# Output stores issued by ACT, attention's ACT work pinned behind the FFN's, the x split pinned on ACT and DVE, and the local part moved in two reading transfers

## The chip, the cores and the metric

One core of one Trainium2 chip runs one program. Its five engines work beside each other, each through a list of its own: TensorE (PE) multiplies, VectorE (DVE), ScalarE (ACT) and GpSimd (POOL) work on elements, SyncE (SP) issues the transfers. The metric is device time in microseconds of one execution, the median of the runs; lower is better.

## The reference

The input is q, k, v of shape (8, 8, 576, 64) and the weights of an FFN. Attention has a far and a local part, whose sum is the FFN's input.

```
q_d, k_d, v_d = mean of q, k, v over groups of 4 positions        # 144 positions
out_up    = repeat(softmax(q_d k_d^T / 8) v_d, 4)                 # far part
out_local = softmax(q k^T / 8 where |i - j| < 4) v                # local part
x = (out_up + out_local) as 4608 tokens x 512
h = x @ w_in ; r = max(h, 0) ; g = s * r*r + b ; out = g @ w_out   # 512 -> 2048 -> 512
```

All of it is float32. The kernel splits x, both weights and g into a high and a low part, and makes each product of three matmuls: high by high, low by high, high by low.

## The kernel before, in words

**Tiles and steps.** The 4608 tokens are 18 tiles of 256, the hidden dimension is 8 parts of 256. One pair (tile t, part p) is a step; from tile 3 on, tile t's steps are numbers 8t to 8t+7. A step has four pieces of work: G (`products1`, L771), 24 matmuls of x by w_in into one bank `ph`, of which the first reads `xh` and the second `xl`; R (`upper`, L786 to L788) on ACT, relu, square and the high part `gh`; V (`lower`, L793) on DVE, the low part `gl`; and H (`products2`, L852 to L854), 12 matmuls into the accumulators `po`. In the third of three steps gh and gl are halves of one tile named `gb`. V reads `ph` last, and from tile 3 on two banks take turns, so G of step k+2 can begin only when V of step k is done. At a tile's end `evict_half` (L826) reads `po` on DVE into `os`, and a store (L829) goes out on SP.

**Stages.** A written list (`PLAN`) sets the order up to step 27 and holds the attention of the first three batches. From step 28 on a loop takes steps in pairs: three matmuls of G, H pieces, the rest of G, R and V (`finish`), one H piece, `advance`, then the whole G of the odd step, its R and V, and six H pieces (18 matmuls), `advance`, and `split`. PE's own order is chained by hand. `advance` pulls as many yields from the attention of batches 3 to 7 as the step number asks (`NY` is the number of yields of a batch), and `split_x` (L752 on ACT, L753 on DVE) writes `xh` and `xl` of tile t+1; it is called after step 8t+5.

**What orders the rest.** A scheduler gives each engine its list, by program order, priorities (`tc.high_priority`) and its own timeline. `behind(engine)` adds one bond: the engine's instructions in the block stand after the last one that the program had issued to that engine, or after a named one. Each engine then works through its list in the listed order.

**Attention of batches 3 to 7.** `two_pairs` makes the local part of two pairs of heads in two halves: seven times POOL multiplies (`pr`, L672) and DVE adds up (`st`, L674), then a softmax (L683 to L691, its exponential L687 on ACT), then seven weighted sums (`pv` L701 on DVE, `acc` L702 on POOL or DVE). The result is turned on DVE (`ft`, L712), written to DRAM (`away`), read back in another layout, and added to x by POOL (L730). Beside it `far_chain` makes the far part: sums over groups of four on DVE (`qd` L529, `kd` L531), three score matmuls on PE (`sa`, L577), the row maximum (`dmx`, L588), exponentials (L589 to L591), a sum (L595), its reciprocal (L596), the scaling (L598), a turn through DRAM (L605 to L620, tile `pd`), three matmuls (`up`, L547 and L549), and a copy into x on ACT (L552).

Of the kernel before, what the change touches and what calls it, by code (L numbers as in the profile page):

```python
# [11 lines left out]
F32 = mybir.dt.float32  # L12
# [74 lines left out]
def attention_ffn_kernel(ctx, tc, qk, vw_in, vr_in, vdm, qkn, vn, w_in, w_out, s_in, b_in, out):  # L87
# [24 lines left out]
    def bank(i, shape, name):  # L112
        return ps.tile(shape, F32, tag=f"k{i}", name=name)
# [442 lines left out]
    def far_chain(units, banks):  # L556

        held = None
        for b, hp in units:
            kd = begin_far(b, hp)  # L560
            yield
            with tc.high_priority(), behind(nc.tensor.engine, chain_end):
                spread = held and end_far(*held, banks)
                scores = far_scores(kd, banks)
            if held:
                spread()
            held = b, hp, (yield from far_rest(b, hp, scores))
            yield
        with behind(nc.tensor.engine, chain_end):
            spread = end_far(*held, banks)  # L570
        spread()
# [8 lines left out]
    def far_rest(b, hp, sa):  # L580

        tmp = lambda shape, name, tag: one.tile(shape, F32, tag=tag, name=name)
        n = 2 * GQ
        dmx = tmp([P, 2, NQ], "dmx", "dmx")[0:n]
        both = tmp([P, NQ * SD], "pd", "pd")
        pd = both[0:n].rearrange("p (i k) -> p i k", i=NQ)
        dsm = tmp([P, NQ], "dsm", "dsm")[0:n]
        nc.vector.tensor_reduce(dmx[:, 0], sa, AX.X, ALU.max, negate=True)  # L588
        nc.scalar.mul(dmx[:, 1], dmx[:, 0], SCALE / 16)  # L589
        for i in range(NQ):  # L590
            nc.scalar.activation(  # L591
                pd[:, i], sa[:, i], AF.Exp, bias=dmx[:, 1, i : i + 1],
                scale=SCALE / 16, accum_out=dsm[:, i : i + 1])
        yield
        nc.scalar.activation(dsm, dsm, AF.Identity, bias=eps[0:n], scale=4.0)  # L595
        nc.vector.reciprocal(dsm, dsm)  # L596
        for i in range(NQ):
            nc.scalar.mul(pd[:, i], pd[:, i], dsm[:, i : i + 1])  # L598
        yield


        away = {}
        for k0, w, tag in ((0, 3, "ptm"), (KM, 2, "vt")):
            ft = tmp([n, w, n], "ft", tag)
            nc.vector.transpose(  # L605
                ft.rearrange("p w (h i c) -> p w i h c", h=2, i=NQ),
                pd[:, :, k0 : k0 + 32 * w].rearrange("p i (w h c) -> p w i h c", w=w, h=2))
            away[k0] = far_off.tile([n, w, n], F32, name="away")
            nc.sync.dma_start(away[k0], ft)
        pm = both[0:KM, 0 : 3 * n].rearrange("p (r n) -> p r n", r=3)  # L610
        pr = both[:, 3 * n : 3 * SD].rearrange("p (r n) -> p r n", r=3)
        for w in range(3):
            m = min(32, KM - 32 * w)
            nc.sync.dma_start(
                pm[32 * w : 32 * w + m],
                away[0][:, w].rearrange("(r a) n -> a r n", r=3)[0:m])
        for h in range(2):
            for w in range(2):
                at = 64 * h + 32 * w
                nc.sync.dma_start(  # L620
                    pr[at : at + 32],
                    away[KM][:, w, GQ * h : GQ * h + GQ].rearrange("(r a) n -> a r n", r=3))
        yield
        return both
# [25 lines left out]
    def two_pairs(b, g, dn):  # L650

        at = GROUPS.index((b, g))
        i = 0

        def far():
            nonlocal i
            if i % 3 == 2:
                next(dn)
            if i == 17:
                load_far(2 * at + 2, ("qk",))  # L660
            i += 1

        acc = None
        st = bank(7, [P, 2, P], "st")
        for h in range(2):
            half = 2 * at + h
            lqk, lv = near_in[half, "lqk"], near_in[half, "lv"]
            ls = take(st[:, h], 0, [P, CH, NO])
            sums = st[:, h, 64 : 64 + CH]
            for o in range(NO):  # L670
                pr = two.tile([P, CH, D], F32, tag="pl", name="pr")
                nc.gpsimd.tensor_tensor(  # L672
                    pr, lqk[:, 0:CH], lqk[:, CH + o : 2 * CH + o], ALU.mult)
                nc.vector.tensor_reduce(ls[:, :, o], pr, AX.X, ALU.add)  # L674
                if o == NO - 1:
                    load_near(half + 1, "lqk")
                    far_values(half)
                    while late:
                        late.pop()()
                far()  # L680
                yield
            row = lambda t: t.unsqueeze(2).to_broadcast([P, CH, NO])
            nc.vector.tensor_tensor(ls, ls, omask, ALU.add)  # L683
            lr = two.tile([P, 2, CH], F32, tag="lr", name="lr")
            nc.vector.tensor_reduce(lr[:, 0], ls, AX.X, ALU.max)
            nc.vector.tensor_tensor(ls, ls, row(lr[:, 0]), ALU.subtract)
            nc.scalar.activation(ls, ls, AF.Exp, scale=SCALE)  # L687
            nc.vector.tensor_reduce(sums, ls, AX.X, ALU.add)
            nc.vector.tensor_scalar(sums, sums, 1e-9, None, ALU.add)
            nc.vector.reciprocal(lr[:, 1], sums)  # L690
            nc.vector.tensor_tensor(ls, ls, row(lr[:, 1]), ALU.mult)  # L691
            far()
            yield
            acc = acc or two.tile([P, CH, 2, D], F32, tag="qk", name="acc")
            for o in range(NO):
                w = ls[:, :, o : o + 1].to_broadcast([P, CH, D])
                if o == 0:
                    nc.vector.tensor_tensor(acc[:, :, h], lv[:, 0:CH], w, ALU.mult)
                else:
                    pv = two.tile([P, CH, D], F32, tag="pv", name="pv")  # L700
                    nc.vector.tensor_tensor(pv, lv[:, o : o + CH], w, ALU.mult)  # L701
                    (nc.vector if o % 3 == 1 else nc.gpsimd).tensor_tensor(  # L702
                        acc[:, :, h], acc[:, :, h], pv, ALU.add)
                if o == NO - 1:
                    load_near(half + 1, "lv")
                far()
                yield
        x = xt[b]
        moved, away = [], []
        for h in range(2):  # L710
            ft = two.tile([P, 2, CH * 32], F32, tag="pv", name="ft")
            nc.vector.transpose(  # L712
                ft.rearrange("p e (i b) -> p e i b", i=CH),
                acc[:, :, h].rearrange("p i (e a) -> p e i a", e=2))
            moved.append(ft)
            away.append(far_off.tile([P, 2, CH * 32], F32, name="away"))
            nc.sync.dma_start(away[h], ft)
        load_far(2 * at + 3, ("qk",))
        yield
        for u in range(2):  # L720
            for e in range(4):
                nc.sync.dma_start(  # L722
                    moved[u][32 * e : 32 * e + 32],
                    away[e // 2][64 * u : 64 * u + 64, e % 2].rearrange("(r a) n -> a r n", r=2))
        yield

        def add():
            for u in range(2):
                xv = x[:, 2 * g + u].rearrange("p (r b i) -> p r b i", r=2, b=32)
                nc.gpsimd.tensor_tensor(  # L730
                    xv, moved[u].rearrange("p r (i b) -> p r b i", i=CH), xv, ALU.add)
            complete.update((b, 2 * g + u) for u in range(2))

        late.append(add)
        yield
# [4 lines left out]
    def split_x(t):  # L740
# [4 lines left out]
        while t0 < (t + 1) * TB:  # L745
            b = t0 // S
            while (b, HP - 1) not in complete:
                next(gen)
            n = min((t + 1) * TB, (b + 1) * S) - t0
            src = xt[b][:, :, t0 - b * S : t0 - b * S + n]  # L750
            dst = slice(t0 - t * TB, t0 - t * TB + n)
            nc.scalar.copy(xh[:, :, dst], src)  # L752
            nc.vector.tensor_tensor(  # L753
                xl[:, :, dst], src, xh[:, :, dst].bitcast(F32), ALU.subtract)
# [66 lines left out]
    def evict_half(t, m):  # L821
# [4 lines left out]
        nc.vector.scalar_tensor_tensor(  # L826
            os_[:, m], oacc[t][m], sb_s, bias, ALU.mult, ALU.add)
# [346 lines left out]
```

## Time and profile before

| | |
|---|---|
| median of 3 runs | 943.72 us (942.95 to 945.33) |
| profiled execution: its time, its span | 944.6 us, 942.8 us |
| mean granted TensorE clock | 0.995 |
| busy: PE, DVE, ACT, POOL | 96%, 69%, 49%, 48% of the span |
| last use of L674 and L701 (attention's end) | near 760 us |
| transfers | 105.09 MB, 111 GB/s on average |

A row of a group names line, engine, operation and tiles, then busy time and the mean of one instruction, then the engine's idle time ahead of these and what ended it. A row of the timeline has start, duration, engine, line, and in brackets the idle time ahead. In a table of stretches each engine has its busy time and its number of instructions, then the granted clock. PE's busy time is modelled from pipelined matmuls, so a full PE can still hide short delays; the distance from one matmul's start to the next shows them.

### The profile page before, as it was taken

Reading aid. Unit: us, or ns where it says so; the run is one execution under the profiler, and the core shown is the slowest. Engines: PE = TensorE matmul, PEld = TensorE weight load, DVE = VectorE, ACT = ScalarE, POOL = GpSimd, SP = SyncE. Lnnn points to the kernel's source line nnn. Section 1 sums busy time; section 2 is a strip of 40 time slices with the busy share of each in tenths; the row PEclk is TensorE's granted clock in tenths of the full one; section 3 lists DMA queues with packets and bytes.
Section 4 is the critical chain, followed back from the end, with each engine's and each line's share of the span. In section 5 each row is a group of like instructions: output and inputs, shape, how many; then the busy total and the mean of one; then the engine's idle time right before and its main releaser. Section 6 shows DMA issues by size and latency. Waiting matters only on the chain.

```text
span 942.8 us, 18601 instructions
## 1 busy us (share of the span) xinstructions
PE 908.2 (96%) x7106; PEld 815.3 (86%) x7106; DVE 654.9 (69%) x1134; ACT 463.6 (49%) x1073; POOL 451.8 (48%) x461
## 2 busy tenths in 40 slices
PE   6799999999999998999999999999999999999998
PEld 5688888788899888999988988989998989999997
DVE  9999999854588887887888778777968672111111
ACT  7977774466455534454544344345534443233331
POOL 6401120010467878687887677768886831000000
PEclk9999999999999999999999999999999999999999
DMA  9855413123234535434443435154434310000000
GB/s 315 279 163 193 148 47 120 46 88 98 90 113 132 157 100 158 131 118 131 138 148 99 146 101 167 56 181 125 144 100 161 85 61 26 23 1 24 1 23 23
DMA packets 60505, 105.09 MB, mean 111 GB/s; under 512 B 20480, under 2 KB 34048, under 8 KB 60416
## 3 DMA queue, kind: packets, MB, share of 16 engines
q1 hardware_dynamic: 60416, 103.90, 35.1%
q8 instruction: 56, 0.92, 0.4%
q14 instruction: 33, 0.27, 0.1%
HBM read 84.85 MB, written 19.02 MB: 110 GB/s over the span
## 4 chain that ended last, share of the span: by engine, by line
PE 42%; POOL 21%; DVE 15%; DMA 12%; issue 5%; ACT 3%; SPq 2%; DVEq 0%; POOLq 0%; ACTq 0%
PE ph L771 19%; POOL pr L672 11%; POOL acc L702 7%; PE po L852 6%; PE po L853 6%; PE po L854 6%; DMA lqk<-in_qkn_dram 4%; DVE pv L701 2%; DMA tqk<-in_qk_dram 2%; DVE st L674 2%; DMA away<-ft 2%; SPq L722 1%; DVE acc L702 1%; PE ol L481 1%; DMA ft<-away 1%
## 5 line engine op out<-in xcount | busy, mean ns | idle before, releaser
L771 PE MATMUL ph<-xh,wi 128*128 128x256 f32 x2176 | 412.6, 280 | 7.3 <-DVE gl L793 3.9
L771 PEld LDWEIGHTS ph<-xh,wi 128*128 128x128 f32 x2176 | 346.3, 189 | 18.0 <-DVE gl L793 6.1
L771 PE MATMUL ph<-xl,wi 128*128 128x256 f32 x1152 | 321.2, 279 | 0.2
L672 POOL TENSOR_TENSOR pr<-lqk 128x576 f32<-128x576 f32 x140 | 203.9, 1478 | 68.2 <-DMA lqk<-in_qkn_dram 44.3
L771 PEld LDWEIGHTS ph<-xl,wi 128*128 128x128 f32 x1152 | 218.8, 190 | 7.8 <-DVE xl L911 0.4
L786 ACT ACTIVATE ph<-ph 128x512 f32<-128x512 f32 x144 | 83.7, 581 | 258.3 <-PE ph L771 252.7
L852 PE MATMUL po<-wo,gh 128*128 128x512 f32 x416 | 166.7, 401 | 0.3
L854 PE MATMUL po<-wo,gl 128*128 128x512 f32 x416 | 163.1, 392 | 0.8 <-DVE gl L793 0.7
L853 PE MATMUL po<-wo,gh 128*128 128x512 f32 x416 | 163.4, 393 | 0.0
L674 DVE TENSOR_REDUCE st<-pr 128x9 f32<-128x576 f32 x140 | 105.6, 754 | 45.4 <-POOL pr L672 43.9
L702 POOL TENSOR_TENSOR acc<-acc,pv 128x576 f32<-128x576 f32 x80 | 114.7, 1433 | 40.0 <-DVE acc L702 22.7
L793 DVE TENSOR_TENSOR gl<-ph,gh 128x512 fp32r<-128x512 f32 x104 | 70.9, 682 | 85.5 <-ACT gh L788 85.5
L701 DVE TENSOR_TENSOR pv<-lv,st 128x576 f32<-128x576 f32 x120 | 87.8, 747 | 25.7 <-POOL acc L702 21.6
L314 POOL TENSOR_TENSOR dq<-vt 80x64 f32<-80x64 f32 x58 | 21.8, 388 | 174.4 <-PE up L385 172.9
L854 PEld LDWEIGHTS po<-wo,gl 128*128 128x128 f32 x416 | 78.3, 188 | 19.2 <-DVE gl L793 2.1
L852 PEld LDWEIGHTS po<-wo,gh 128*128 128x128 f32 x416 | 78.2, 188 | 13.3 <-issue 0.8
L853 PEld LDWEIGHTS po<-wo,gh 128*128 128x128 f32 x416 | 78.5, 189 | 11.4 <-issue 0.2
L787 ACT ACTIVATE ph<-ph 128x512 f32<-128x512 f32 x144 | 83.8, 582 | 4.0
L788 ACT CAST gh<-ph 128x512 fp32r<-128x512 f32 x104 | 61.1, 587 | 20.3 <-PE po L853 18.2
L852 PE MATMUL po<-wo,gb 128*128 128x512 f32 x160 | 63.2, 395 | 2.9 <-DVE os L826 1.7
L853 PE MATMUL po<-wo,gb 128*128 128x512 f32 x160 | 62.9, 393 | 0.0
L854 PE MATMUL po<-wo,gb 128*128 128x512 f32 x160 | 62.5, 391 | 0.0
(175 smaller groups left out, 1188.4 us busy)
## 6 DMA issues: line engine op xcount, KB each, us to landing
tqk<-in_qk_dram SPq DMA_DIRECT2D x30, 584.0 KB, 4.3
lqk<-in_qkn_dram SPq DMA_DIRECT2D x20, 768.0 KB, 4.4
lv<-in_vn_dram SPq DMA_DIRECT2D x20, 480.0 KB, 3.5
out_dram<-os SPq DMA_DIRECT2D x34, 256.0 KB, 2.1
wst<-in_moe_w_in_dram SPq DMA_DIRECT2D x7, 1024.0 KB, 5.8
wst<-in_moe_w_out_dram SPq DMA_DIRECT2D x7, 1024.0 KB, 5.1
away<-ft SPq DMA_DIRECT2D x20, 288.0 KB, 2.8
ft<-away SPq DMA_DIRECT2D x80, 72.0 KB, 2.0
```

What stands on the lines that cost most here:

```text
L672: nc.gpsimd.tensor_tensor(pr, lqk[:, 0:CH], lqk[:, CH + o : 2 * CH + o], ALU.mult)
L674: nc.vector.tensor_reduce(ls[:, :, o], pr, AX.X, ALU.add)
L701: nc.vector.tensor_tensor(pv, lv[:, o : o + CH], w, ALU.mult)
L702: (nc.vector if o % 3 == 1 else nc.gpsimd).tensor_tensor(acc[:, :, h], acc[:, :, h], pv, ALU.add)
L771: nc.tensor.matmul(ph[:, j], wi[p][:, s, k, f], xk[:, k], start=k == 0 and s == 0 and xk is xh, stop=k == NK - 1 and s == 1)
L786: nc.scalar.activation(ph, ph, AF.Relu)
L787: nc.scalar.activation(ph, ph, AF.Square)
L788: nc.scalar.copy(gh, ph)
L793: nc.vector.tensor_tensor(gl, acc.pop((t, p)), gh.bitcast(F32), ALU.subtract)
L852: nc.tensor.matmul(po[m], gh[:, j, ms], wo[p][:, 0, j], start=first, stop=False)
L853: nc.tensor.matmul(po[m], gh[:, j, ms], wo[p][:, 1, j], start=False, stop=False)
L854: nc.tensor.matmul(po[m], gl[:, j, ms], wo[p][:, 0, j], start=False, stop=last)
```

## The change

- Output stores of tiles 2 to 16 are queued (`to_store`) and issued on ACT, in the next `finish`, behind that step's R. The last tile's stores stay on SP.
- In the far part the negated row maximum stays where it was, and a slot later come the exponentials and the sum, pinned on ACT behind what was issued there last; the scaling comes another slot later, pinned too. The score matmuls are pinned behind PE's last issued ones. The number of slots per unit of the far part stays five.
- The local part's exponential is a slot later and pinned on ACT. A pair of pairs now takes 32 slots for its two halves (30 before), and `NY` goes from 34 to 36.
- `split_x`: `xh` is pinned on ACT and `xl` on DVE behind what was issued there last.
- The turned result is written to DRAM in four transfers for each half, the first half's in the middle of the second half, and read back in two transfers of 128 partitions. Before, it was two writes and eight reads of 32 partitions at the end.

```diff
@@ far_chain
-                scores = far_scores(kd, banks)
+                with behind(nc.tensor.engine):
+                    scores = far_scores(kd, banks)
...
             held = b, hp, (yield from far_rest(b, hp, scores))
-            yield
@@ far_rest
         nc.vector.tensor_reduce(dmx[:, 0], sa, AX.X, ALU.max, negate=True)
-        nc.scalar.mul(dmx[:, 1], dmx[:, 0], SCALE / 16)
-        for i in range(NQ):
-            nc.scalar.activation(...Exp...)
-        yield
-        nc.scalar.activation(dsm, dsm, AF.Identity, bias=eps[0:n], scale=4.0)
+        yield
+        with behind(nc.scalar.engine):
+            nc.scalar.mul(dmx[:, 1], dmx[:, 0], SCALE / 16)
+            for i in range(NQ):
+                nc.scalar.activation(...Exp...)
+            nc.scalar.activation(dsm, dsm, AF.Identity, bias=eps[0:n], scale=4.0)
         nc.vector.reciprocal(dsm, dsm)
-        for i in range(NQ):
-            nc.scalar.mul(pd[:, i], pd[:, i], dsm[:, i : i + 1])
+        yield
+        with behind(nc.scalar.engine):
+            for i in range(NQ):
+                nc.scalar.mul(pd[:, i], pd[:, i], dsm[:, i : i + 1])
@@ two_pairs
-            if i % 3 == 2:
+            if i % 3 == 2 and i < 30:
                 next(dn)
...
+        away = far_off.tile([4, P, CH * 32], F32, name="away")
+        def turn(h):
+            ft = two.tile([P, 2, CH * 32], F32, tag="pv", name="ft")
+            nc.vector.transpose(...)
+            for r in range(4):
+                nc.sync.dma_start(
+                    away[r, 64 * h : 64 * h + 64].rearrange("(e a) n -> a e n", e=2),
+                    ft[32 * r : 32 * r + 32])
...
+                if h == 1 and o == 2:
+                    turn(0)
...
-            nc.scalar.activation(ls, ls, AF.Exp, scale=SCALE)
+            far()
+            yield
+            with behind(nc.scalar.engine):
+                nc.scalar.activation(ls, ls, AF.Exp, scale=SCALE)
...
         for u in range(2):
-            for e in range(4):
-                nc.sync.dma_start(moved[u][32 * e : 32 * e + 32], ...)
+            moved.append(two.tile([P, 2, CH * 32], F32, tag="pv", name="moved"))
+            nc.sync.dma_start(moved[u], away[2 * u : 2 * u + 2].rearrange("r p n -> p r n"))
@@ split_x
-            nc.scalar.copy(xh[:, :, dst], src)
-            nc.vector.tensor_tensor(
-                xl[:, :, dst], src, xh[:, :, dst].bitcast(F32), ALU.subtract)
+            with behind(nc.scalar.engine):
+                nc.scalar.copy(xh[:, :, dst], src)
+            with behind(nc.vector.engine):
+                nc.vector.tensor_tensor(
+                    xl[:, :, dst], src, xh[:, :, dst].bitcast(F32), ALU.subtract)
@@ evict_half
-        nc.sync.dma_start(out[r0 : r0 + P, :], os_[:, m])
+        to_store.append(((nc.sync if t < 2 else nc.scalar), out[r0 : r0 + P, :], os_[:, m]))
...
-    NY = [10 * HP] * NE + [34 * (HP // 2)] * (B - NE)
+    NY = [10 * HP] * NE + [36 * (HP // 2)] * (B - NE)
@@ finish
+        ready = len(to_store)
         with tc.high_priority():
             next(streams["R"])
             next(streams["V"])
+            with behind(nc.scalar.engine):
+                store(ready)
```

The engines' lists are the same up to about step 28. Three places after it follow. In the changed kernel G is L784, H L874 to L876, R L799 to L801, V L806, the x split L764 and L766; of attention L674 is L689, L683 to L686 are L700 to L703, L688 to L691 are L708 to L711, L698 is L718, L701 is L721, L702 is L722, L712 is L672, L595 and L596 are L596 and L597.

On DVE, the low part of x for tile 12 (`xl_8059` before, `xl_8086` now; its first reader is step 96). Before it stands between V of step 86 (`ph_7417`) and V of step 87:

```order
L702 TENSOR_TENSOR acc_7259<-acc_7259,pv_7641 128x9x64
L793 TENSOR_TENSOR gb_7445<-ph_7417,gb_7445 128x512
L701 TENSOR_TENSOR pv_7650<-lv_7480,st_7065 128x576
L701 TENSOR_TENSOR pv_7698<-lv_7480,st_7065 128x576
L753 TENSOR_TENSOR xl_8059<-x_6141,xh_8058 128x1024
L793 TENSOR_TENSOR gl_7514<-ph_7488,gh_7513 128x512
```

Now it stands behind V of step 95 (`ph_8162`), with ten instructions of attention between them:

```order
L806 TENSOR_TENSOR gb_8187<-ph_8162,gb_8187 128x512
L721 TENSOR_TENSOR pv_7971<-lv_7740,st_7791 128x576
L722 TENSOR_TENSOR acc_7918<-acc_7918,pv_7968 128x9x64
L721 TENSOR_TENSOR pv_8020<-lv_7740,st_7791 128x576
L689 TENSOR_REDUCE st_7791<-pr_8025 128x9
L689 TENSOR_REDUCE st_7791<-pr_8028 128x9
L672 STREAM_TRANSPOSE ft_8060<-acc_7918 128x576
L689 TENSOR_REDUCE st_7791<-pr_8057 128x9
L689 TENSOR_REDUCE st_7791<-pr_8066 128x9
L588 TENSOR_REDUCE dmx_8081<-sa_8076 96x3
L531 TENSOR_REDUCE kd_8340<-tqk_8037 128x144
L766 TENSOR_TENSOR xl_8086<-x_6149,xh_8085 128x1024
```

It moved nine steps later, from well ahead of its reader to the last step before it. Tiles 5, 9 and 14 have moved in the same way: their `xl` stands behind V of steps 39, 71 and 111. Those of the other tiles stand behind V of the sixth step of the tile before, and one piece of tile 6 behind the seventh.

On PE, the end of the H pieces after step 95 and the beginning of step 96 (`ph_8244` before, `ph_8248` now). Before:

```order
L852 MATMUL po_7792<-wo_1557,gh_8011 128x512
L853 MATMUL po_7792<-wo_1557,gh_8011 128x512
L854 MATMUL po_7792<-wo_1557,gl_8012 128x512
L771 MATMUL ph_8244<-xh_8058,wi_466 128x256
L771 MATMUL ph_8244<-xl_8059,wi_466 128x256
```

Now:

```order
L876 MATMUL po_7797<-wo_1557,gl_8015 128x512
L547 MATMUL up_8072<-pd_7863,dq_160 128x144
L549 MATMUL up_8072<-pd_7863,dq_160 128x144 x2
L577 MATMUL sa_8076<-kd_8032,dq_160 96x144 x3
L784 MATMUL ph_8248<-xh_8085,wi_466 128x256
L784 MATMUL ph_8248<-xl_8086,wi_466 128x256
```

The matmuls of one unit of the far part have moved in ahead of step 96; the order of G and H is the same.

On ACT, around the high part of x for tile 12. Before, the copy `xh_8058` stands inside R of step 87 (`ph_7488`), and the far part's copy follows that R:

```order
L788 CAST gb_7445<-ph_7417 128x512
L786 ACTIVATE ph_7488<-ph_7488 128x512
L752 CAST xh_8058<-x_6141 128x1024
L787 ACTIVATE ph_7488<-ph_7488 128x512
L788 CAST gh_7513<-ph_7488 128x512
L552 COPY x_7557<-up_7558 128x576
```

Now it stands behind the whole R of step 95 and a copy that waits for `up`:

```order
L801 CAST gb_8187<-ph_8162 128x512
L552 COPY x_7567<-up_8072 128x576
L764 CAST xh_8085<-x_6149 128x1024
L535 COPY dq_160<-qd_8339 64x9x16 x2
L591 ACTIVATE dmx_8081<-dmx_8081 96x3
L593 ACTIVATE pd_8082,dsm_8083<-sa_8076,dmx_8081 96x144 x3
L596 ACTIVATE dsm_8083<-dsm_8083,eps_164 96x3
```

R is no longer divided by the copy of x, and attention's ACT work stands between two whole Rs.

More of the change, by code (lines that the diff above doesn't have):

```diff
@@ L588, in far_rest @@
         nc.vector.tensor_reduce(dmx[:, 0], sa, AX.X, ALU.max, negate=True)
-        nc.scalar.mul(dmx[:, 1], dmx[:, 0], SCALE / 16)
-        for i in range(NQ):
-            nc.scalar.activation(
-                pd[:, i], sa[:, i], AF.Exp, bias=dmx[:, 1, i : i + 1],
-                scale=SCALE / 16, accum_out=dsm[:, i : i + 1])
-        yield
-        nc.scalar.activation(dsm, dsm, AF.Identity, bias=eps[0:n], scale=4.0)
+        yield
+        with behind(nc.scalar.engine):
+            nc.scalar.mul(dmx[:, 1], dmx[:, 0], SCALE / 16)
+            for i in range(NQ):
+                nc.scalar.activation(
+                    pd[:, i], sa[:, i], AF.Exp, bias=dmx[:, 1, i : i + 1],
+                    scale=SCALE / 16, accum_out=dsm[:, i : i + 1])
+            nc.scalar.activation(dsm, dsm, AF.Identity, bias=eps[0:n], scale=4.0)
         nc.vector.reciprocal(dsm, dsm)
-        for i in range(NQ):
-            nc.scalar.mul(pd[:, i], pd[:, i], dsm[:, i : i + 1])
+        yield
+        with behind(nc.scalar.engine):
+            for i in range(NQ):
+                nc.scalar.mul(pd[:, i], pd[:, i], dsm[:, i : i + 1])
         yield
@@ L664, in two_pairs @@
         st = bank(7, [P, 2, P], "st")
+        away = far_off.tile([4, P, CH * 32], F32, name="away")
+        def turn(h):
+            ft = two.tile([P, 2, CH * 32], F32, tag="pv", name="ft")
+            nc.vector.transpose(
+                ft.rearrange("p e (i b) -> p e i b", i=CH),
+                acc[:, :, h].rearrange("p i (e a) -> p e i a", e=2))
+            for r in range(4):
+                nc.sync.dma_start(
+                    away[r, 64 * h : 64 * h + 64].rearrange("(e a) n -> a e n", e=2),
+                    ft[32 * r : 32 * r + 32])
         for h in range(2):
@@ L708, in two_pairs @@
         x = xt[b]
[L709 to L717, printed above, removed]
+        turn(1)
         load_far(2 * at + 3, ("qk",))
         yield
+        moved = []
         for u in range(2):
-            for e in range(4):
-                nc.sync.dma_start(
-                    moved[u][32 * e : 32 * e + 32],
-                    away[e // 2][64 * u : 64 * u + 64, e % 2].rearrange("(r a) n -> a r n", r=2))
+            moved.append(two.tile([P, 2, CH * 32], F32, tag="pv", name="moved"))
+            nc.sync.dma_start(moved[u], away[2 * u : 2 * u + 2].rearrange("r p n -> p r n"))
         yield
@@ L828, in evict_half, with store @@
         r0 = TB * t + P * m
-        nc.sync.dma_start(out[r0 : r0 + P, :], os_[:, m])
+        to_store.append(((nc.sync if t < 2 else nc.scalar), out[r0 : r0 + P, :], os_[:, m]))
+        if t < 2:
+            store(1)
+    to_store = []
+    def store(count):
+        for _ in range(count):
+            engine, dst, src = to_store.pop(0)
+            engine.dma_start(dst, src)
     def evict(t):
```

## The prediction

> **What bounds the kernel now.** I read the head of the page first, then a table of stretches: the attention stage from G of step 32 to G of step 112, a pair of steps in the tail, and two windows in which the clock fell.
>
> ```profile
> PE 908.2 (96%) x7106; PEld 815.3 (86%) x7106; DVE 654.9 (69%) x1134; ACT 463.6 (49%) x1073; POOL 451.8 (48%) x461
> ...
> 270.13:755.64 485.51, 473.68 (x3109) 430.29 (x3108) 385.77 (x670) 219.73 (x535) 377.04 (x337) 0.99 0.42 128
> 805.46:816.42 10.96, 10.96 (x75) 9.97 (x74) 2.89 (x4) 3.50 (x7) 0.00 (x0) 1.00 0.13 49
> 369.76:373.17 3.41, 3.41 (x19) 3.41 (x18) 3.27 (x9) 0.00 (x0) 1.48 (x2) 0.50 0.83 265
> 622.35:625.75 3.40, 3.40 (x14) 3.11 (x15) 3.22 (x6) 0.00 (x0) 2.85 (x3) 0.50 0.75 243
> ```
>
> PE is the bound. A pair of steps with nothing beside it takes 10.96 us, so the 40 pairs of the stage need 438.4 of their 485.5. PE also has the far part's matmuls there, 20 units. The timeline shows one:
>
> ```profile
> 321.25 0.48 PE L547 MATMUL up<-pd,dq 128*128 128x144 f32 x2 [0.73 <-ACT ph L786]
> ...
> 322.06 0.90 PE L577 MATMUL sa<-kd,dq 128*96 128x144 f32 x6
> 322.71 0.49 PE L852 MATMUL po<-wo,gb 128*128 128x512 f32 x1
> ```
>
> From 321.25 to 322.71 are 1.46 us, times 20 are 29.2. That leaves 17.9 us in which PE is held up: all that a better order can win in this stage, plus some 1.5 us at its edges. Who holds it, from the waits of PE between 250 and 765 us (sum, times, longest):
>
> ```profile
> PE ph L771 <- DVE gl L793: 3.9, 3, 2.3
> PE ph L771 <- ACT xh L752: 2.6, 1, 2.6
> PE po L852 <- DVE os L826: 1.7, 1, 1.7
> PE up L547 <- ACT ph L786: 1.4, 2, 0.7
> PE po L852 <- DVE dsm L596: 1.2, 1, 1.2
> PE up L547 <- DMA pd<-away: 0.6, 1, 0.6
> PE ph L771 <- DVE gb L793: 0.6, 1, 0.6
> ```
>
> These 12.0 us are late V (a bank not free), one late x split, late evictions and late far parts. The two longest, 2.6 and 2.3, stand ahead of the two windows at half clock above, which cost 1.7 us each. The rest is what PE takes to come back up after each wait.
>
> **The x split: the term that decides.** A new tile can't begin without its `xl`. How long PE has between the last G of a tile and the first of the next, and when V comes in between, shows in the tail, at an odd step:
>
> ```profile
> 807.91 0.28 PE L771 MATMUL ph<-xh,wi 128*128 128x256 f32 x1
> ...
> 808.22 0.58 ACT L786 ACTIVATE ph<-ph 128x512 f32<-128x512 f32 x1 [1.60 <-PE ph L771]
> ...
> 810.12 0.59 ACT L788 CAST gh<-ph 128x512 fp32r<-128x512 f32 x1 [0.70 <-PE po L853]
> ...
> 810.74 0.69 DVE L793 TENSOR_TENSOR gl<-ph,gh 128x512 fp32r<-128x512 f32 x1 [3.39 <-ACT gh L788]
> ...
> 812.13 0.28 PE L771 MATMUL ph<-xh,wi 128*128 128x256 f32 x1
> ```
>
> I count from G's last matmul, 807.91: gh is ready at +2.8, V at +3.5 at the earliest, and PE wants the next x at +4.2. Now `xl` of tiles 5, 9, 12 and 14 stands behind V of the step just before, with attention between. What these instructions take, from DVE's groups and then ACT's in the attention stage:
>
> ```profile
> L674 DVE TENSOR_REDUCE st<-pr 128x9 f32<-128x576 f32 x140 | 105.6, 754 | 45.4 <-POOL pr L672 43.9
> L701 DVE TENSOR_TENSOR pv<-lv,st 128x576 f32<-128x576 f32 x116 | 84.9, 747 | 25.5 <-POOL acc L702 21.4 <-POOL x L730 3.5
> L702 DVE TENSOR_TENSOR acc<-acc,pv 128x576 f32<-128x576 f32 x39 | 39.4, 1010 | 1.2 <-POOL acc L702 1.2
> L531 DVE TENSOR_REDUCE kd<-tqk 128x144 f32<-128x576 f32 x20 | 14.8, 739 | 0.0
> L712 DVE STREAM_TRANSPOSE ft<-acc 128x576 f32<-128x576 f32 x18 | 13.8, 765 | 0.1
> L588 DVE TENSOR_REDUCE dmx<-sa 96x3 f32<-96x432 f32 x20 | 11.9, 595 | 0.2 <-PE sa L577 0.2
> L753 DVE TENSOR_TENSOR xl<-x,xh 128x1024 fp32r<-128x1024 f32 x7 | 10.5, 1502 | 0.5 <-ACT xh L752 0.5
> L691 DVE TENSOR_TENSOR st<-st,lr 128x63 f32<-128x63 f32 x20 | 4.6, 230 | 0.6
> L596 DVE RECIPROCAL dsm<-dsm 96x3 f32<-96x3 f32 x20 | 3.3, 164 | 2.0 <-ACT dsm L595 1.9
> ...
> L591 ACT ACTIVATE pd<-sa,dmx 96x144 f32<-96x144 f32 x60 | 22.0, 372 | 1.7
> L591 ACT ACTIVATION_READ_ACCUMULATOR pd<-sa,dmx 96x1 f32 x60 | 11.6, 194 | 0.0
> L552 ACT COPY x<-up 128x576 f32<-128x576 f32 x20 | 12.9, 643 | 18.7 <-PE up L549 18.7
> L752 ACT CAST xh<-x 128x1024 fp32r<-128x1024 f32 x7 | 7.3, 1042 | 0.8 <-POOL x L730 0.8
> L595 ACT ACTIVATE dsm<-dsm,eps 96x3 f32<-96x3 f32 x20 | 6.0, 298 | 0.5
> L589 ACT ACTIVATE dmx<-dmx 96x3 f32<-96x3 f32 x20 | 4.1, 206 | 41.4 <-DVE dmx L588 41.2
> ```
>
> In the old names, between V and `xl`:
> - Tile 12: 2 L701, 1 L702, 4 L674, 1 turn, L588, L531 = 1.49 + 1.01 + 3.02 + 0.77 + 0.60 + 0.74 = 7.6. The turn also waits for the last two POOL additions of its half, and the L674 behind it for POOL's next products; I follow these in POOL's list and add 2.1. 3.5 + 7.6 + 2.1 + 1.5 for xl = 14.7. PE has 1.46 of far matmuls in its gap, so it wants xl at 5.7: it waits 9.0.
> - Tile 14: 5 L674, L588, L596. Here L596 waits for ACT: `sa` ends at 5.7, L588 6.3, L589 6.6 (ACT is held until 6.7 by L552 and xh), so 6.9; three exponentials at 0.57 make 8.6, L595 8.9, L596 9.1, two L674 10.6, xl 12.1. Minus 5.7: 6.4.
> - Tile 5: L674, 7 small ones at 0.2, the local exponential on ACT between them 0.3, 3 at 0.75, L596 = 5.0; 3.5 + 5.0 + 1.5 = 10.0, minus 4.2: 5.8.
> - Tile 9: 3 L701, L702, L588, L531, 2 L674 = 6.1; 3.5 + 6.1 + 1.5 = 11.1. The far matmuls stand behind the new tile's first one, so PE waits from 5.8: 5.3.
>
> Sum 26.5 us. Low ends, without POOL's and ACT's waits, L702 at 0.75 and xl at 1.2, as if each had no neighbour: 6.4, 3.5, 5.2, 4.7, sum 19.8. High ends: tile 9 waits for POOL too (1.5), tile 14 one product longer (0.9), and tile 6's last piece, which needs POOL's addition, up to 3: 32. A wait of 2.3 and one of 2.6 cost 1.7 of clock; I take 4 times 1.7 = 6.8, with ends 0 and 13.6 (two windows each). The Trainium skill, "TensorE: Matmul & The Clock Gate", Part 1 on the clock gate, holds that it takes about an idle window of 3.4 us to fall to half and warns of PE gaps over that. The windows here are 3.41 long as it says, but the trace falls after 2.3, which decides. By that page the four waits at these sizes would trip it too, so its sum is the same.
>
> The same reading of the list of before names one tile, 6, whose xh comes last, and the trace has just that wait:
>
> ```profile
> 365.64 1.70 POOL L730 TENSOR_TENSOR x<-ft,x 128x576 f32<-128x576 f32 x1
> ...
> 367.37 1.35 ACT L752 CAST xh<-x 128x256 fp32r<-128x256 f32 x2 [2.97 <-POOL x L730]
> ...
> 367.83 0.38 PE L771 MATMUL ph<-xh,wi 128*128 128x256 f32 x1 [2.59 <-ACT xh L752]
> ```
>
> **The other parts.**
> - Exponentials and scaling a slot later, behind R. Before, ACT stood 41.2 us ahead of L589 waiting for the maximum, with R queued behind it. Now the maximum is long done. Late V goes as far as ACT made it late; DVE's share stays. Of 3.9 + 0.6 I let half stay (2.2), the eviction's 1.7 stay, and DMA's 0.6. So 4.5 of the 17.9 remain and 13.4 go, the two slow windows and the late far parts (matmuls placed later in PE's list) among them. Ends: 6 and all 19.4 with the edges.
> - Behind the pinned ACT work queue DVE's L596 and L688. They wait longer, which delays the next V. The list puts other work ahead of them except at tile 14, where it is counted. Elsewhere no two neighbouring Vs have over 10 us between them, within what two banks allow. So 0, up to 3.
> - Stores: 30 from ACT at the 0.36 us that their issue took on SP are 10.7 us, at two per tile behind a finished R. ACT is half idle and the rows come a step after the eviction, so 0; SP's list loses 30 entries.
> - Local part: ten transfers a pair of pairs stay ten, half of the writes earlier. Adding to x comes perhaps 2 us sooner. It is hidden, except at tile 6, where it is part of the xh term above. POOL runs beside PE, and attention ends 180 us before the FFN.
> - `NY` and slots: 35 yields of 36 instead of 33 of 34, the same pace: 0.
>
> Sum: 944.6 (the profiled time, 0.9 above the median) - 13.4 + 26.5 + 6.8 = 964.5, so 963.6 for the median. I say 963.
>
> **Rivals.**
> - The old waits stay. DVE and not ACT makes V late, so only about 5 of the 17.9 go: 943.7 - 5 + 33.3 = 972. For it: DVE and POOL are near 80% busy in the stage. Against it: 41.2 us of ACT waits ahead of R, and DVE catches up whenever PE stands.
> - The waits are short: the low ends, 19.8, with the clock falling at two of four (3.4), and 17 won: 943.7 - 17 + 23.2 = 950. For it: neighbouring instructions of DVE can begin before the one ahead has ended. Against: tile 14 waits for a chain over three engines.
> - Faster, on the other side: DVE's queue at the four boundaries drains in half the time, as PE's pause frees POOL and memory for it. With 17.9 won, the point is 17.9 / 4 = 4.5 us a boundary, clock included. At 3.7 each: 943.7 - 17.9 + 14.8 = 940.6. Against: V alone at +3.5 and xl at 1.2 give 0.5 before any of the seven to ten instructions between, and their durations are a mean of many.
> - The edits cancel: within 0.3% (2.8 us, about what this measurement can tell from no change), the same at 4.5 us a boundary.
>
> **How the numbers follow.** The likeliest case (955 to 968) has 0.68, the old waits 0.15, the short waits 0.10, faster 0.04, the same 0.03. All but the last two are slower: 0.93. From the short waits' 950 up to the old waits' 972, with some room above for two windows a boundary: 950 to 974.
>
> **What would show it.** At G of steps 40, 72, 96 and 112, PE waits 4 to 9 us for DVE `xl`, the four longest waits of the profile, each followed by a window at half clock; 20 to 32 us in all. ACT's wait ahead of the far part's first ACT instruction (L589 before) falls from 41 us to under 15, and waits of G for `gl` to under 3. ACT issues 30 stores without idle time ahead. I am wrong if these four waits are under 3 us, if `xl` runs ahead of its V, or if PE's other waits were worth more than 17.9.

## The result and the profile after

The changed kernel took 975.44 us (median of 4 runs, 974.63 to 979.36), the kernel before 943.9 beside it: 1.034 times as long, with a 95% interval of 1.031 to 1.037. I had said 963, with 950 to 974. The sign and the four places were right; the waits there were too small in my sum.

The profiled execution took 974.88 us, 30.3 more than that of before. The head of its page, and then PE's waits over the whole span (sum, times, longest):

```profile
PE 914.0 (94%) x7106; PEld 821.2 (84%) x7106; DVE 652.6 (67%) x1134; ACT 465.7 (48%) x1073; POOL 450.2 (46%) x461
```

```profile
PE ph L784 <- DVE xl L766: 16.3, 4, 6.7
PE up L547 <- DMA pd<-away: 11.6, 4, 4.6
...
PE ph L784 <- ACT xh L764: 7.3, 3, 6.1
```

DVE, ACT and POOL do the same work as before in a longer span. The waits of G for `gl` and for `gb` are gone from the list, as are those for evictions. In their place stand the split, and far parts (`pd`) that come late.

The stretches below reach from the last G matmul of step 39, 71, 95 and 111 to that of step 41, 73, 97 and 113. Then come, one in each, the stretches in which the clock was at half. The columns are the length, the busy time and number of instructions of PE, its weight loads, DVE, ACT and POOL, the granted clock, and the share and rate of the transfers.

```profile
312.61:335.10 22.49, 14.28 (x75) 12.48 (x73) 16.96 (x28) 7.36 (x19) 15.54 (x11) 0.77 0.28 89
512.08:537.09 25.01, 16.45 (x86) 14.65 (x85) 16.99 (x26) 5.11 (x11) 20.93 (x19) 0.73 0.38 107
663.59:687.71 24.12, 16.55 (x87) 14.39 (x86) 20.40 (x37) 8.46 (x22) 17.93 (x17) 0.79 0.43 125
769.04:793.24 24.20, 15.07 (x87) 13.16 (x85) 18.70 (x34) 7.91 (x20) 15.65 (x15) 0.86 0.24 63
```

```profile
321.10:331.30 10.20, 6.10 (x24) 5.52 (x25) 9.23 (x13) 2.93 (x9) 6.78 (x5) 0.50 0.29 112
519.10:532.70 13.60, 7.56 (x29) 6.90 (x30) 9.40 (x13) 1.26 (x3) 12.71 (x13) 0.50 0.30 83
672.70:682.90 10.20, 7.21 (x27) 6.22 (x28) 7.99 (x12) 4.82 (x15) 9.42 (x11) 0.50 0.49 157
781.90:788.70 6.80, 4.05 (x16) 3.77 (x17) 5.76 (x15) 1.13 (x4) 0.77 (x1) 0.50 0.09 27
```

Without loss each stretch would take 10.96 us, and the last three 1.46 more for a unit of the far part. So the four lose 95.82 - 43.84 - 4.38 = 47.6 us. From G of step 32 to G of step 114, 41 pairs and 20 units, before took 498.1 us (270.1 to 768.2) and after 528.3 (269.9 to 798.2). Without loss it would be 478.6: 19.5 were lost before, 49.7 after, of which 47.6 at the four places and 2.1 elsewhere. The 30.2 us are thus 47.6 new, less 17.4 won.

The timeline around G of step 72, PE's rows and then DVE's, shows the largest of the four:

```profile
516.30 0.28 PE L784 MATMUL ph<-xh,wi 128*128 128x256 f32 x1
520.41 0.82 PE L547 MATMUL up<-pd,dq 128*128 128x144 f32 x2 [3.83 <-DMA pd<-away]
...
528.36 0.58 PE L784 MATMUL ph<-xl,wi 128*128 128x256 f32 x1 [4.73 <-DVE xl L766]
```

```profile
515.98 0.68 DVE L806 TENSOR_TENSOR gb<-ph,gb 128x512 fp32r<-128x512 f32 x1
520.12 0.75 DVE L721 TENSOR_TENSOR pv<-lv,st 128x576 f32<-128x576 f32 x1 [3.46 <-POOL acc L722]
521.60 0.86 DVE L722 TENSOR_TENSOR acc<-acc,pv 128x576 f32<-128x576 f32 x1 [0.73 <-POOL acc L722]
...
523.66 0.60 DVE L588 TENSOR_REDUCE dmx<-sa 96x3 f32<-96x432 f32 x1 [0.54 <-PE sa L577]
...
527.09 1.21 DVE L766 TENSOR_TENSOR xl<-x,xh 128x1024 fp32r<-128x1024 f32 x1
```

PE reads `xh`, then stands for `pd` and for `xl` in turn. Behind V at 515.98, DVE stands 3.46, 0.73 and 0.54 us for POOL and for PE itself. That last wait leads back to PE: the far matmuls stand between the first and the second matmul of step 72, `dmx` waits for them, and `xl`, which the second matmul needs, is queued behind `dmx`.

At step 40 PE stands longer for `xh` than for `xl`. The pinned `xh` stands on ACT behind the exponentials of the local and the far part, the first of which stood 4.71 us for DVE:

```profile
323.09 0.58 PE L784 MATMUL ph<-xh,wi 128*128 128x256 f32 x1 [6.10 <-ACT xh L764]
325.78 0.58 PE L784 MATMUL ph<-xl,wi 128*128 128x256 f32 x1 [2.11 <-DVE xl L766]
```

### The profile page after: what moved, and what is told of

Its sections match the earlier page's. It is cut to its first block, busy times and chain, and to the rows that moved or that the text cites. A ratio compares the mean times of both kernels' runs of the same rounds, so it can differ in the third digit from the quotient of the medians.

```text
span 972.7 us, 18562 instructions
## 1 busy us (share of the span) xinstructions
PE 914.0 (94%) x7106; PEld 821.2 (84%) x7106; DVE 652.6 (67%) x1134; ACT 465.7 (48%) x1073; POOL 450.2 (46%) x461
## 4 chain that ended last, share of the span: by engine, by line
PE 59%; POOL 15%; DVE 14%; DMA 6%; issue 3%; ACT 2%; SPq 1%; DVEq 0%; POOLq 0%; ACTq 0%
PE ph L784 27%; PE po L874 9%; PE po L875 9%; PE po L876 9%; POOL pr L687 7%; POOL acc L722 5%; DMA lqk<-in_qkn_dram 2%; DVE pv L721 2%; PE ol L481 1%; DMA away<-ft 1%; POOL x L741 1%; DVE bias L822 1%; DVE acc L722 1%; DVE st L689 1%; PE sa L577 1%
## 5 line engine op out<-in xcount | busy, mean ns | idle before, releaser
L784 PE MATMUL ph<-xh,wi 128*128 128x256 f32 x2176 | 414.2, 281 | 7.3 <-ACT xh L764 7.3
L784 PEld LDWEIGHTS ph<-xh,wi 128*128 128x128 f32 x2176 | 348.1, 190 | 16.8 <-ACT xh L764 8.3
L784 PE MATMUL ph<-xl,wi 128*128 128x256 f32 x1152 | 322.9, 280 | 17.4 <-DVE xl L766 16.3
L784 PEld LDWEIGHTS ph<-xl,wi 128*128 128x128 f32 x1152 | 219.5, 191 | 26.4 <-DVE xl L766 17.7
L799 ACT ACTIVATE ph<-ph 128x512 f32<-128x512 f32 x144 | 83.8, 582 | 286.6 <-PE ph L784 281.5
L874 PE MATMUL po<-wo,gh 128*128 128x512 f32 x416 | 166.8, 401 | 0.0
L876 PE MATMUL po<-wo,gl 128*128 128x512 f32 x416 | 163.8, 394 | 1.4 <-DVE gl L806 1.2
L689 DVE TENSOR_REDUCE st<-pr 128x9 f32<-128x576 f32 x140 | 106.0, 757 | 59.4 <-POOL pr L687 57.8
L806 DVE TENSOR_TENSOR gl<-ph,gh 128x512 fp32r<-128x512 f32 x104 | 71.1, 684 | 109.3 <-ACT gh L801 102.8
L722 POOL TENSOR_TENSOR acc<-acc,pv 128x576 f32<-128x576 f32 x80 | 116.6, 1458 | 52.1 <-DVE acc L722 38.8
L314 POOL TENSOR_TENSOR dq<-vt 80x64 f32<-80x64 f32 x58 | 20.7, 367 | 174.4 <-PE up L385 173.0
L721 DVE TENSOR_TENSOR pv<-lv,st 128x576 f32<-128x576 f32 x120 | 87.3, 747 | 18.4 <-POOL acc L722 17.5
L876 PEld LDWEIGHTS po<-wo,gl 128*128 128x128 f32 x416 | 78.7, 189 | 19.8 <-DVE gl L806 2.6
L874 PEld LDWEIGHTS po<-wo,gh 128*128 128x128 f32 x416 | 78.7, 189 | 12.6 <-issue 0.2
L801 ACT CAST gh<-ph 128x512 fp32r<-128x512 f32 x104 | 61.1, 588 | 27.9 <-PE po L875 25.7
L874 PE MATMUL po<-wo,gb 128*128 128x512 f32 x160 | 62.8, 392 | 0.0
L876 PE MATMUL po<-wo,gb 128*128 128x512 f32 x160 | 62.4, 390 | 0.0
```

The source lines that it names most:

```text
L722: (nc.vector if o % 3 == 1 else nc.gpsimd).tensor_tensor(acc[:, :, h], acc[:, :, h], pv, ALU.add)
L784: nc.tensor.matmul(ph[:, j], wi[p][:, s, k, f], xk[:, k], start=k == 0 and s == 0 and xk is xh, stop=k == NK - 1 and s == 1)
L799: nc.scalar.activation(ph, ph, AF.Relu)
L801: nc.scalar.copy(gh, ph)
L806: nc.vector.tensor_tensor(gl, acc.pop((t, p)), gh.bitcast(F32), ALU.subtract)
L874: nc.tensor.matmul(po[m], gh[:, j, ms], wo[p][:, 0, j], start=first, stop=False)
```

## The experiments

Each ratio is to the kernel before on the same chip, with its 95% interval. "Lost" is the sum, from 250 us on, of each matmul's distance to the next over the median distance for the same two lines: 24.9 us in before, 54.8 in the changed kernel. Where the text says what a step lost, it is the part of this sum at that step. The chips differ a little (before took 943.9 to 946.5 on them), so runs of different groups are best compared by their ratios.

| run | median, us | ratio (95%) | lost, us |
|---|---|---|---|
| changed, split not pinned | 941.6 | 0.9945 (0.993 to 0.996) | 18.4 |
| changed, split pinned behind R and V | 952.7 | 1.0070 (1.005 to 1.009) | 29.8 |
| before + the split's pins | 950.7 | 1.0045 (1.003 to 1.006) | 29.7 |
| changed, far part as before | 982.0 | 1.0373 (1.036 to 1.039) | 61.5 |
| changed, only xl pinned | 976.5 | 1.0341 (1.031 to 1.037) | 54.4 |
| changed, only xh pinned | 962.6 | 1.0191 (1.017 to 1.022) | 39.1 |
| before + far part | 941.2 | 0.9959 (0.994 to 0.997) | 20.7 |
| changed, no pins, no slot | 935.3 | 0.9893 (0.986 to 0.992) | 16.4 |
| before + far part + turn | 944.3 | 0.9995 (0.998 to 1.001) | 18.8 |
| before + far part + stores | 944.2 | 0.9995 (0.998 to 1.001) | 20.1 |
| before + stores | 944.3 | 0.9987 (0.997 to 1.001) | 24.1 |
| before + stores + turn | 945.2 | 1.0000 (0.999 to 1.001) | 21.2 |
| changed, no slot, pins stay | 949.8 | 1.0042 (1.003 to 1.006) | 29.7 |
| before + pins + slot | 968.5 | 1.0231 (1.021 to 1.025) | 48.2 |

**The split not pinned.**

```diff
-            with behind(nc.scalar.engine):
-                nc.scalar.copy(xh[:, :, dst], src)
-            with behind(nc.vector.engine):
-                nc.vector.tensor_tensor(xl[:, :, dst], ...)
+            nc.scalar.copy(xh[:, :, dst], src)
+            nc.vector.tensor_tensor(xl[:, :, dst], ...)
```

> The changed kernel with the two pins of the x split taken away; all else stays. xl of tiles 5, 9, 12 and 14 stands then behind V of steps 30, 65, 86 and 102, one to ten steps ahead of its reader's. Theory P (the pins alone put xl in the last step before its reader, and the 46.3 us that PE loses at steps 40, 72, 96 and 112 are their price): those four stretches lose under 3 us each apart from waits of the far matmuls for pd, which stood for 11.6 us; instead xl of tile 6 now stands behind nine instructions in step 47, five of them reductions at POOL's pace of 1.5 us: 3.5 + 7.5 + 0.7 + 1.2 - 4.2 = 8.8 us at step 48, with clock 10.5. So 975 - 46 + 10.5 + 0 to 12 = 939 to 952. Theory Q (the attention work runs late through its own slots and transfers, and PE stops at a tile's start whatever the split's place, for far parts and x): at least 30 of the 46 us stay, 960 to 975.

It took 941.6, 34 us less than the changed kernel (37 by the ratios) and 0.55% faster than before. PE's waits from 250 to 765 us:

```profile
PE ph L782 <- ACT xh L763: 9.7, 1, 9.7
PE up L547 <- ACT ph L798: 1.2, 1, 1.2
PE up L547 <- DMA pd<-away: 0.4, 1, 0.4
PE up L547 <- POOL acc L722: 0.2, 1, 0.2
```

The waits for `xl` are gone, and so are those for `pd` but for 0.4 us, though the far part's slots are unchanged. In the changed kernel's list the far matmuls stood at the beginnings of steps 72, 96 and 112; without the pins they stand elsewhere (70, 73, 98, 115). One stall is left, tile 6 at step 48, which loses 12.2 of the 18.4. In the changed kernel step 48 loses 0.2. Theory P held, Q fell.

**Pinned behind R and V of its own step.** One added line is put in words.

```diff
             next(streams["R"])
             next(streams["V"])
+            fin[:] = the last ACT and the last DVE instruction issued
...
-            with behind(nc.scalar.engine):
+            with behind(nc.scalar.engine, fin[0]):
...
-            with behind(nc.vector.engine):
+            with behind(nc.vector.engine, fin[1]):
```

> The changed kernel, with the split pinned behind R and V of its own step instead of behind whatever the program issued last to ACT and DVE (which is attention's). xl stands right behind V of steps 37, 69, 93 and 109, three steps ahead of its reader; tile 6's second piece behind seven instructions in step 47, three of them reductions. Theory P: what costs is not a pin but that it ties xl to attention's last instruction; the waits for xl at steps 40, 72, 96 and 112 go, at step 48 some 5 us and 1.7 of clock come, so 975 - 46 + 7 + 0 to 12 for pd = 936 to 948. Theory Q: 960 to 975. A third, D (DVE has no room: xl ahead of attention moves the lateness to V or to POOL's partners): waits of G for gl come back, of over 5 us in all, 950 to 960.

It took 952.7. PE's waits in the same stretch:

```profile
PE ph L785 <- ACT xh L765: 8.5, 2, 7.5
PE up L547 <- DMA pd<-away: 4.8, 5, 1.8
PE up L547 <- ACT ph L801: 1.4, 1, 1.4
PE ph L785 <- DVE xl L767: 0.3, 1, 0.3
```

The four places are clean, as P said (0.7 us lost at step 72, nothing at the others), and step 48 loses 10.8. But the time is above P's 936 to 948: five waits for `pd`, and after 765 us one of 2.8 for an eviction on DVE, were in no theory. It lies in D's range, but no wait for `gl` appears, so D's mechanism isn't it. Perhaps a split that is placed early pushes attention back in smaller pieces; no run shows that.

**The pins alone, and the slot.** The first run adds the split's pins to the kernel before:

> The kernel before with the two pins of the split alone. xl of tiles 5, 9, 12 and 14 stands behind V of steps 37, 69, 93 and 111, the last with one reduction between. Theory P in its strict form (pins alone cost 40 us): over 970. In the form that I hold, pins cost only where attention's last issued instruction is itself late in DVE's list, which takes the slots that the change has added: here only step 112 (3.5 + 0.8 + 1.5 - 5.7, nothing to 1 us) and tile 6 at step 48, with five small instructions between: 943.9 + 0 to 5 = 944 to 949. Theory Q: 943 to 946, since pins do nothing.

It took 950.7, just above what I held, and far from the strict form: step 112 lost 5.7 us, where I had 1 at most, and step 41, which I hadn't named, 6.2. So the pins need something beside them. Two later runs ask whether that is the local part's later slot. The edit taken away from the changed kernel in one and added to the pins in the other:

```diff
-            if i % 3 == 2 and i < 30:
+            if i % 3 == 2:
...
-            far()
-            yield
-            with behind(nc.scalar.engine):
-                nc.scalar.activation(ls, ls, AF.Exp, scale=SCALE)
+            nc.scalar.activation(ls, ls, AF.Exp, scale=SCALE)
...
-    NY = [10 * HP] * NE + [36 * (HP // 2)] * (B - NE)
+    NY = [10 * HP] * NE + [34 * (HP // 2)] * (B - NE)
```

> The changed kernel with the split pinned as it is and without the local part's later slot (34 slots a unit again). xl of tiles 5, 9, 12 and 14 stands behind V of steps 39, 69, 93 and 110, the first with a reciprocal and one addition between, the last with four instructions. Theory Sl (the pins cost what they do because the added slot makes attention's last DVE instruction a step or two later): only step 40 still waits, 3.5 + 0.2 + 1.0 + 1.5 - 4.2 = 2 us, with V late up to 4, and its clock 1.7 to 3; so 935.3, which is the same without pins, and 2 to 10: 937 to 947. Theory Fa (it is the far part's two added slots, here still in place): 960 to 976.

> The kernel before with the split's pins and the local part's later slot; the far part, the turn and the stores as before. xl stands behind V of steps 39, 71, 93 and 111 with two, ten, seven and six instructions between; at step 112 six reductions at POOL's pace. Theory Sl: step 72 waits 10 us, step 112 10, step 40 3, with clock 5 to 8 in all, on top of the pins' 950.7: 966 to 980. Theory Fa: 948 to 955, as with the pins alone.

They took 949.8 and 968.5. With the pins and the slot alone, PE's long waits are back (250 to 800 us):

```profile
PE ph L776 <- DVE xl L758: 22.3, 3, 11.7
PE ph L776 <- ACT xh L756: 3.8, 1, 3.8
PE up L547 <- DMA pd<-away: 3.4, 2, 2.8
```

Fa fell in both; Sl held in the second and was 3 us too low in the first. In the kernel before the pins cost 4 us, and pins and slot together 22; the slot without the pins was not run there, so its own share of the 22 is not known. In the changed kernel the pins cost 14 without the slot (949.8 against 935.3, further down) and 34 with it (975.4 against 941.6), while the slot alone costs 5 to 6 (941.6 against 935.3). So most of the loss is what the two make together, and the rest of the change adds some. In that run without the slot step 40 lost 7.6, within the 2 to 10 of its sum, but one far part came 5.2 us late at step 65, which lost 8.4.

**Without the far part's edits.** The five edits in `far_chain` and `far_rest` are undone, all else stays.

> The changed kernel with the far part as before (exponentials in the maximum's slot, nothing of it pinned); the split's pins, the local part's slot and transfers and the stores stay. xl of tiles 5, 9 and 14 stands behind V of steps 39, 71 and 111 still, behind 5, 8 and 12 instructions, and tile 12's behind V of step 93. Theory P: three boundaries still cost 8 to 12 us each, step 96 none, and ACT's waits for the maximum are back, which takes most of the 16 us won elsewhere: 943.9 + 3 x 10 - 0 to 8 = 966 to 974. A rival, F (the far part's added slots are what fills DVE and the far matmuls' waits, so without them the boundaries are cheap): 945 to 955.

It took 982.0, so rival F fell and my own range was too low: steps 40 and 72 lost 7.2 and 10.0, but step 112 alone 16.8, and step 48, which my sum left out, 8.0. At step 112 `xl` stood behind twelve instructions, seven of them reductions, of which five stood 0.6 us each for POOL's product.

**One pin at a time.**

```diff
-            with behind(nc.scalar.engine):
-                nc.scalar.copy(xh[:, :, dst], src)
+            nc.scalar.copy(xh[:, :, dst], src)
             with behind(nc.vector.engine):
```

> The changed kernel with only the pin of xl on DVE; xh on ACT is free and stands nine to sixteen steps earlier for tiles 9 and 12. xl stands behind V of steps 39, 71, 95 and 111 with nine, eight, eight and eight instructions between. Theory P-DVE (it is xl on DVE, tied to attention's last instruction, that PE waits for): the four stretches still cost 9 to 12 us each, 40 in all, so 970 to 978. Theory P-ACT (the pinned xh comes late, behind attention's exponentials and the copy of the far part, and xl only follows it): with xh early the four stretches cost under 4 each, 940 to 955.

```diff
-            with behind(nc.vector.engine):
-                nc.vector.tensor_tensor(xl[:, :, dst], ...)
+            nc.vector.tensor_tensor(xl[:, :, dst], ...)
```

> The changed kernel with only the pin of xh on ACT. xl, free on DVE but behind its xh by the data, stands behind V of steps 39, 95 and 111 with thirteen, eleven and four instructions between; tile 9's behind V of step 69 with one. Theory P-DVE: the stretch at step 72 costs nothing now, that at 112 some 6 us in place of 10, those at 40 and 96 stay at 11 to 12: 975 - 13 - 4 = 955 to 962. Theory P-ACT: all four stay, 970 to 978.

The pin on DVE alone costs as much as both: 976.5. With the pin on ACT alone step 72 loses 0.1 us, step 112 7.3, steps 40 and 96 10.6 and 13.3, which is P-DVE's pattern; the time of 962.6 is just over its range. But it is still 21 us above the run without pins: at steps 40 and 96 the pin of `xh` alone is enough to make `xl` late, since `xl` reads `xh`. Either pin does it there, at step 72 only that of `xl`, and at step 112 that of `xh` does half.

**Where the gain is from.** The far part's edits alone:

```diff
+        yield
+        with behind(nc.scalar.engine):
+            nc.scalar.mul(dmx[:, 1], dmx[:, 0], SCALE / 16)
...
```

> The kernel before with the far part alone changed (exponentials and scaling a slot later, pinned; score matmuls pinned). My step on this part: ACT no longer stands for the maximum ahead of R, so V comes sooner and 12 to 16 us of the 17.9 in the attention stage go, with tile 6's x still late at step 48: 930 to 936. Rival: it takes the local part's and the stores' changes as well to win that, and the far part alone gives under 5: 939 to 946.

It gave 4 us, not 12 to 16. ACT's wait ahead of the far part went as forecast, from 41.2 to 3.8 us from 250 to 765 us (the changed kernel has 5.0):

```profile
L591 ACT ACTIVATE dmx<-dmx 96x3 f32<-96x3 f32 x20 | 4.0, 201 | 4.1 <-DVE dmx L588 3.8
```

And PE still waits for V there:

```profile
PE ph L774 <- DVE gl L796: 2.1, 2, 1.3
PE ph L774 <- ACT xh L755: 2.1, 1, 2.1
...
PE ph L774 <- DVE gb L796: 1.3, 2, 0.8
```

Of the 4.5 us of waits for `gl` and `gb` 3.4 are left. So ACT's standing was not what most of the late V hung on. The changed kernel without pins and without the slot:

> The changed kernel without the pins of the split and without the later slot of the local part's exponential (34 slots again). The far part, the turn in two reading transfers and the stores stay. Theory S (with the pins away, what is left at step 48 is x of batch 3 coming late, because the local part's two added slots push its turn back): tile 6's xl now stands right behind V of step 47, the wait at step 48 falls from 9.7 us to 0 to 3, and the time from 941.6 by 8 to 11 to 930 to 934. Rival (the slot is what kept ACT free, and without it R comes late again): waits of G for gl come back by 5 to 8, and the time stays at 936 to 943.

It took 935.3, the fastest of all and 1.1% under before; its interval is far from 1. PE's waits for the stage:

```profile
PE up L547 <- DMA pd<-away: 3.3, 3, 2.1
PE ph L779 <- ACT xh L760: 1.3, 1, 1.3
PE ph L779 <- DVE xl L761: 0.8, 1, 0.8
```

The wait at step 48 fell from 9.7 to 2.1, as S said, and no wait for V is left; the time is 1 us above S's range and below its rival's. Four runs ask which of the stores and the turn goes with the far part; their edits are parts of the diff above, the first with

```diff
+            moved.append(two.tile([P, 2, CH * 32], F32, tag="pv", name="moved"))
+            nc.sync.dma_start(moved[u], away[2 * u : 2 * u + 2].rearrange("r p n -> p r n"))
```

> The kernel before with the far part changed and the result turned in two reading transfers; no pins of the split, no later slot, stores on SP. The far part alone gave 941.2, with turn and stores 935.3. Theory T (the turn brings x and its buffers sooner, which is the other 6 us): 934 to 938. Theory St (30 stores off SP's list let the inputs and pd come sooner, which is the other 6 us): 940 to 943.

the second with

```diff
-        nc.sync.dma_start(out[r0 : r0 + P, :], os_[:, m])
+        to_store.append(((nc.sync if t < 2 else nc.scalar), out[r0 : r0 + P, :], os_[:, m]))
```

> The kernel before with the far part changed and the stores on ACT. Theory St: 934 to 938. Theory T: 940 to 943.

> The kernel before with the stores on ACT and nothing else. My step put this at 0, so 944 to 946.5 beside a before of 945.3. Theory St: stores alone already give 3 to 6 us, 939 to 943. A cost is possible too: a store issued on ACT stands behind R for its tile's eviction and delays the next R, 946 to 950.

> The kernel before with the stores on ACT and the turn in two reading transfers, the far part as before. If the far part's pins are what the gain rests on (ACT standing 41 us for the maximum ahead of R), these two give under 2 us by themselves, 943 to 946. If they work alone, by T or St, 938 to 941.

None differs from before: 944.3, 944.2, 944.3 and 945.2. Far part and turn, and far part and stores, are even 3 us above the far part alone (0.9995 both, against 0.9959). T and St both fell. Only all three together give 10 us, and that is no sum of their parts. Each edit makes the scheduler lay DVE's and PE's lists anew, and a few waits of 1 to 3 us come or go with that; what in the three together removes them stays open.

## Why the prediction was right or wrong

- **The places were right.** `xl` of tiles 5, 9, 12 and 14 was late as read from the list of the changed kernel, and the pins are shown as the cause: 975.4 with both, 976.5 with that of `xl` alone, 962.6 with that of `xh` alone, 941.6 with none. What I hadn't seen is that most of it takes the slot as well: 949.8 with both pins and without the slot.
- **The step that failed is the size of the four waits**, 26.5 us with a high end of 32. `xl` ended 13.1, 16.2, 15.6 and 15.6 us after the last G matmul; I had 10.0, 11.1, 14.7 and 12.1. With what I took that PE wants (4.2, 5.8, 5.7, 5.7), that is 39.1 in place of 26.5. Two things were left out. I let V end 3.5 us after G, "at the earliest"; it ended at 4.2, 4.6, 4.2 and 6.9, which is 5.9 us in all. And for tiles 5 and 9 I laid DVE's instructions end to end: DVE stood 2.0 us behind V of step 39 and 4.7 behind that of 71. For tile 12 I had 2.1 of standing, and it was 2.0. For tile 14 the size was near, 3.1 against 2.6, but the wait was another: I had the reciprocal wait for ACT's exponentials, and it stood for nothing; four reductions stood for POOL's products. The late V and the standing, 13 us beyond what I had, make up the missing 12.6. At step 39 DVE stood for POOL, whose two additions to x (L741) stand between its products, one ahead of each of two; DVE's rows and then POOL's, with the second addition:

```profile
315.48 0.76 DVE L689 TENSOR_REDUCE st<-pr 128x9 f32<-128x576 f32 x1 [2.32 <-POOL pr L687]
316.14 0.68 DVE L806 TENSOR_TENSOR gl<-ph,gh 128x512 fp32r<-128x512 f32 x1
318.53 0.76 DVE L689 TENSOR_REDUCE st<-pr 128x9 f32<-128x576 f32 x1 [1.70 <-POOL pr L687]
...
323.43 2.29 DVE L766 TENSOR_TENSOR xl<-x,xh 128x1024 fp32r<-128x1024 f32 x1
```

```profile
315.40 1.74 POOL L741 TENSOR_TENSOR x<-moved,x 128x576 f32<-128x576 f32 x1
317.09 1.40 POOL L687 TENSOR_TENSOR pr<-lqk 128x576 f32<-128x576 f32 x1
```

- **The sign I named** was 20 to 32 us of waits for `xl`. The trace has 16.3, since at the four places PE stands for `xh` (7.2) and for `pd` (9.9) first; together that is 33.4.
- **The clock**: four times 1.7 was near enough. The 47.6 us less 39.1 leave 8.5 in place of 6.8; that is a remainder and not a measurement. At each place the clock was at half for two to four windows of 3.41 us, not one (6.8 to 13.6 us), but these begin while PE still waits, and PE stands in much of them.
- **The gain was too small**: 17.4 of the stretch's 19.5 where I had 13.4. My reason for it isn't shown: ACT's wait went as I said, but the far part's edits alone gave 4. Part of the gain hangs on the loss: with PE late from step 40 on, tile 6's x is in time for step 48, which loses 0.2 us, against 4.9 in before and 12.2 without the split's pins. The larger gain hid 4.0 us of what I had missed in the waits.
- **Late far parts**: I let DMA's 0.6 us stay; it became 11.6. I had them going, with their matmuls placed later in PE's list; three units of them came to stand at the beginnings of steps 72, 96 and 112, and there PE waited 9.9 of the 11.6. It cost little by itself, since the wait for `xl` follows and DVE stood only once, 0.54 us, for these matmuls.
- **Stores, and the turn**, were put at nothing. Stores alone, and stores with the turn, measure as nothing on the kernel before (0.9987 and 1.0000). Beside the far part, turn or stores take some 3 us of its gain and both together add 6, which no term of mine held. "Without idle time ahead" did not quite hold: R stands 4.8 us in all for a store issued ahead of it.

```profile
L799 ACT ACTIVATE ph<-ph 128x512 f32<-128x512 f32 x144 | 83.8, 582 | 286.6 <-PE ph L784 281.5 <-DMA out_dram<-os 4.8
```

In sum, -13.4 + 26.5 + 6.8 = 19.9 was forecast, and -17.4 + 39.1 + 8.5 = 30.2 came. The time is 1.4 us above the range's end. I had taken that end from the rival of the old waits; the high end that I had for the four waits themselves, 32 us, was 7 below what came.

## What to carry to other kernels

A bond "behind what was issued last" ties an instruction to whatever that is: tie it to a named one, or leave it free, if its own reader has a due time. When a wait is priced from a list of instructions, add what each of them waits for on other engines, and let the chain start where it starts in the trace's busy stretches, not at its earliest. Where a scheduler lays the work out anew, edits don't add up: far part, turn and stores together gave 10 us where the far part alone gave 4 and no pair of them as much, and pins that cost 4 alone cost 34 beside the rest.

## What the hardware showed that I had not expected

POOL's rows at steps 40 and 72, two products each, and ahead of the second two undisturbed ones:

```profile
323.24 3.75 POOL L687 TENSOR_TENSOR pr<-lqk 128x576 f32<-128x576 f32 x2 [4.75 <-DMA lqk<-in_qkn_dram]
```

```profile
515.27 2.78 POOL L687 TENSOR_TENSOR pr<-lqk 128x576 f32<-128x576 f32 x2 [7.29 <-DVE acc L722]
...
527.09 3.86 POOL L687 TENSOR_TENSOR pr<-lqk 128x576 f32<-128x576 f32 x2
```

`xl` (rows above) took 2.29 us at step 40, where POOL had begun 0.19 us before it, and 1.21 at step 72, where both began at once; with nothing on POOL beside it, at step 112, it took 1.22. POOL's pair took 3.75 and 3.86 in place of 2.78. The Trainium skill, "SBUF — State Buffer", on the shared port pair, says that a DVE operation with two inputs in SBUF and a POOL operation that reads SBUF exclude each other for a whole instruction, and the later one waits. These rows agree: in the first case `xl` waited some 1.1 us, in both POOL lost about the length of one `xl`.
